# Block 0's causal taps: products summed by TensorE with the identity, halo rows dropped, orders laid out anew

## The chip, the cores and the metric

The kernel runs on one core of a Trainium2 chip, in one launch. The metric is the device time of that core in microseconds. Three runs of the kernel before gave 284.77, 285.18 and 283.43 us, the median 284.77.

The engines that matter are TensorE (PE in the profile: matmuls out of SBUF into PSUM, with PEld for its weight loads), VectorE (DVE: elementwise work), ScalarE (ACT: copies out of PSUM, activations), GpSimd (POOL) and SyncE (SP: it issues nearly all DMAs).

## What is computed

The inputs are q, k, v of 2048 rows by 640 channels, four taps per channel (`shift_k`, 640 by 4), a long filter per channel (`ssm_k`, 640 by 2048) and the weights of a gated feed-forward layer (640 by 1728). Cut to what matters here:

```python
k_shift = jnp.zeros_like(k)
for t in range(ks):                      # ks = 4, k_pad: three zero rows ahead of k
    k_shift = k_shift + k_pad[:, t:t + S, :] * shift_k[:, ks - 1 - t]
kv = k_shift * v                         # the part that the change touches
y = causal_convolution(kv, ssm_k)        # by rfft2/irfft2 in the reference
y = y + kv * ssm_D
h = q + layernorm(q) * y
out = h + (silu(n @ w_gate) * (n @ w_up)) @ w_down      # n = layernorm(h)
```

Row s of `k_shift` is the sum over jj = 0..3 of row s - jj of k times tap jj; rows before the first are zero.

## The kernel before

The 2048 rows are cut into four blocks (j = 0..3) of 512 and the 640 channels into two halves (c = 0, 1) of `CW` = 320. In a block, partition p holds rows 4p to 4p + 3, as four slots b of 320 columns.

For each (j, c), `kv_block` makes the tap sum times v. The k tile of 7 slots holds three halo slots ahead of the four (the last three rows of partition p - 1), so that row 4p + b - jj is slot 3 + b - jj of the same partition. `mul2` forms two taps' products in one VectorE instruction of 2560 columns (`kvn`), `mul1` one of 1280 (`kvs`), `add2` adds 1280 columns (`kva`), and a last multiply by v writes over the v tile (`kvv`). For block 0 the halo comes in two extra transfers per half (`kin0ch`), and GpSimd zeroes the three slots of partition 0 (`kz`).

Block 0 is then convolved by dense matrices: `ktr` turns the filter over on TensorE and `kte` copies it out, `dadd` adds D; `dfK` and `dfX` are eight 320-column matmuls each, for four h per half (the forward transform of the filter and of kv), evacuated by `deK`/`deX` on ScalarE; `m1`, `m2`, `cr`, `ci` are the products on VectorE; `di` (eight matmuls per h) sums the inverse in four PSUM banks; `w` (ScalarE) and `h` (VectorE) form the residual, `bn`, `ag`, `va` and GpSimd's `nr` the second layer norm. Only then come `hn` (the normalised rows), their transposes `tr0` and copies `te0`, and the first feed-forward matmuls `gu0`. Later blocks are convolved in two stages (`s1`, `s2`, `i2`, `i1`), and their first stages are filled in between block 0's work.

The taps: a transfer brings 2560 values into one partition of zeroed rows (`WP`), a matmul with ones spreads them over the partitions (`tapm`, four pairs of 320 columns), and four copies write them to `TAPS` (`tap`). Matmuls on ones (`warm`) and on the identity (`fill`), 512 columns wide, compute nothing; `WARM` and `FILL` say how many.

The program's order is not found at run time: `_PLAN` is a table that gives each operation its engine, its place in that engine's queue and its buffer slots, and for some transfers another one whose landing must be awaited before they are issued. Each engine works strictly through its own queue. PSUM has eight banks; a pair of banks takes one `dfK` or `dfX`, four banks one half's `di`.

## Time and profile before

| | us |
|---|---|
| median of three runs | 284.77 (283.43 to 285.18) |
| the profiled execution's own time | 285.63 |
| its span, first to last instruction | 282.8 |
| TensorE busy in the span | 268.2 (95%) |
| VectorE busy | 232.1 (82%) |
| ScalarE busy | 198.1 (70%) |
| GpSimd busy | 16.0 (6%) |

So 2.8 us of the profiled time lie around the span, and it is 0.86 us above the median. Times below are counted from the span's start. A row of the timeline gives start, length, engine, line, operation and how many instructions are merged, and in brackets the idle time ahead of it and what ended it. A row of a group gives the count, the busy time, the mean duration in ns and the idle time before. Nearly every matmul is issued at line 514, and nearly every VectorE product or sum at line 736, since helpers record them; they are told apart by their tile's shape and their place in the order. A matmul's duration there is its latency: in a row of them the next starts long before the last has ended.

### The profile page before, as it was taken

Reading aid. Unit: us, or ns where it says so; the run is one execution under the profiler, and the core shown is the slowest. Engines: PE = TensorE matmul, PEld = TensorE weight load, DVE = VectorE, ACT = ScalarE, POOL = GpSimd, SP = SyncE. Lnnn points to the kernel's source line nnn. Section 1 sums busy time; section 2 is a strip of 40 time slices with the busy share of each in tenths; the row PEclk is TensorE's granted clock in tenths of the full one; section 3 lists DMA queues with packets and bytes.
Section 4 is the critical chain, followed back from the end, with each engine's and each line's share of the span. In section 5 each row is a group of like instructions: output and inputs, shape, how many; then the busy total and the mean of one; then the engine's idle time right before and its main releaser. Section 6 shows DMA issues by size and latency. Waiting matters only on the chain.

```text
span 282.8 us, 4764 instructions
## 1 busy us (share of the span) xinstructions
PE 268.2 (95%) x1694; PEld 146.5 (52%) x1710; DVE 232.1 (82%) x428; ACT 198.1 (70%) x322; POOL 16.0 (6%) x22
## 2 busy tenths in 40 slices
PE   8989988898999998999999999999999998999996
PEld 2557554355444476644444566544444774444574
DVE  4899999999999998999999999999996843043414
ACT  4458987979989987977999789688998821430100
POOL 3000010200000021100000202000001020000000
PEclk9999999799999999999999999999999999999999
DMA  6896896899966966568432355542012061000013
GB/s 181 252 318 164 250 282 211 259 264 257 275 185 190 314 162 195 119 192 226 141 116 93 109 153 139 163 139 95 0 68 94 27 66 52 0 0 2 0 37 126
DMA packets 55282, 41.84 MB, mean 148 GB/s; under 512 B 20256, under 2 KB 52571, under 8 KB 55260
## 3 DMA queue, kind: packets, MB, share of 16 engines
q1 hardware_dynamic: 55114, 41.51, 50.5%
q8 instruction: 13, 0.21, 0.3%
q14 instruction: 9, 0.07, 0.1%
q10 hardware_dynamic: 146, 0.04, 0.1%
HBM read 19.91 MB, written 2.62 MB: 80 GB/s over the span
## 4 chain that ended last, share of the span: by engine, by line
PE 54%; DVE 26%; DMA 8%; ACT 4%; issue 3%; SPq 2%; POOL 1%; DVEq 0%
PE ps L514 53%; DVE sb L736 21%; DMA sb<-in_A_k_dram 3%; SPq L502 2%; ACT sb L494 2%; DMA sb<-sb 2%; DMA sb<-in_B_w_down_dram 2%; DMA sb<-in_A_ssm_k_dram 1%; POOL stt L863 1%; DVE sb L1066 1%; DVE sb L1228 1%; DVE stt L846 1%; ACT sb L897 1%; ACT L1161 0%; DVE sb L877 0%
## 5 line engine op out<-in xcount | busy, mean ns | idle before, releaser
L514 PE MATMUL ps<-sb 128*128 128x320 bf16 (+2 forms) x1218 | 223.0, 336 | 7.9 <-DVE sb L736 1.5
L736 DVE TENSOR_TENSOR sb<-sb 128x1280 bf16<-128x1280 bf16 (+5 forms) x273 | 180.1, 722 | 4.5 <-ACT sb L494 2.9
L514 PEld LDWEIGHTS ps<-sb 128*128 128x128 bf16 (+1 forms) x1234 | 117.4, 98 | 100.4 <-issue 8.9
L494 ACT ACTIVATE sb<-ps 128x640 bf16<-128x640 f32 (+2 forms) x160 | 112.1, 753 | 23.8 <-PE ps L514 18.8
L514 PE MATMUL ps<-sb,tab 128*128 128x320 bf16 (+2 forms) x432 | 55.2, 307 | 3.4 <-ACT sb L1161 1.0
L1161 ACT ACTIVATE sb<-ps 128x1024 bf16<-128x1024 f32 (+2 forms) x32 | 29.1, 917 | 33.3 <-PE ps L514 33.1
L514 PEld LDWEIGHTS ps<-sb,tab 128*128 128x128 f16 (+2 forms) x432 | 25.8, 102 | 30.3 <-issue 13.6
L736 DVE TENSOR_TENSOR sb<-ps,sb 128x1024 bf16<-128x1024 f32 (+2 forms) x14 | 12.6, 913 | 21.2 <-ACT sb L1161 12.1
L863 POOL TENSOR_TENSOR stt<-stt 128x2 f32<-128x2 f32 (+1 forms) x12 | 13.4, 1117 | 212.7 <-DVE stt L862 203.6
L1062 ACT ACTIVATE sb<-ps,stt 128x320 f32<-128x320 f32 x32 | 17.9, 624 | 3.3 <-PE ps L514 1.8
L1066 DVE SCALAR_TENSOR_TENSOR sb<-sb,stt 128x320 bf16<-128x320 bf16 x32 | 16.5, 543 | 0.4 <-ACT sb L1062 0.4
L1228 DVE SCALAR_TENSOR_TENSOR sb<-ps,stt,sb 128x640 bf16<-128x640 f32 x12 | 10.4, 880 | 5.4 <-PE ps L514 5.2
L897 ACT ACTIVATE sb<-sb,stt 128x640 uint8<-128x640 bf16 x16 | 13.4, 835 | 1.1 <-DVE stt L893 1.1
L890 ACT ACTIVATE sb<-sb 128x640 uint8<-128x640 bf16 x16 | 11.8, 740 | 0.4 <-DMA sb<-in_A_q_dram 0.3
L1203 DVE SCALAR_TENSOR_TENSOR sb<-ps,stt,sb 128x320 bf16<-128x320 f32 x8 | 4.1, 547 | 9.5 <-PE ps L514 9.5
L915 ACT ACTIVATE sb<-sb,stt 128x640 uint8<-128x640 bf16 x12 | 9.9, 827 | 1.2 <-DVE stt L910 0.9
L878 ACT ACTIVATE sb<-sb,stt 128x640 bf16<-128x640 bf16 x8 | 7.2, 916 | 0.3 <-DVE stt L870 0.2
L846 DVE BATCH_NORM_STATS2 stt<-sb 128x6 f32<-128x320 bf16 x8 | 3.7, 477 | 0.0
L877 DVE TENSOR_SCALAR sb<-sb,stt 128x640 bf16<-128x640 bf16 x8 | 3.5, 442 | 0.2 <-DMA sb<-sb 0.2
L495 DVE CAST sb<-ps 128x640 bf16<-128x640 f32 x1 | 0.8, 825 | 3.0 <-PE ps L514 3.0
L897 ACT ACTIVATION_READ_ACCUMULATOR sb<-sb,stt 128x1 f32 x16 | 3.3, 206 | 0.0
L890 ACT ACTIVATION_READ_ACCUMULATOR sb<-sb 128x1 f32 x16 | 3.2, 203 | 0.0
(27 smaller groups left out, 26.2 us busy)
## 6 DMA issues: line engine op xcount, KB each, us to landing
sb<-sb SPq DMA_DIRECT2D x72, 160.0 KB, 2.7
sb<-in_A_k_dram SPq DMA_DIRECT2D x6, 560.0 KB, 4.3
sb<-in_A_v_dram SPq DMA_DIRECT2D x8, 320.0 KB, 4.5
sb<-in_A_q_dram SPq DMA_DIRECT2D x8, 320.0 KB, 3.5
sb<-cst_den SPq DMA_DIRECT2D x8, 256.0 KB, 4.5
sb<-sb SPq DMA_DIRECT2D x24, 80.0 KB, 2.6
out_dram<-sb SPq DMA_DIRECT2D x12, 160.0 KB, 1.9
sb<-in_B_w_down_dram SPq DMA_DIRECT2D x3, 480.0 KB, 5.0
```

What stands on the lines that cost most here:

```text
L494: fns = {"act": lambda a: a.activation(out=dst(), in_=src(), func=ACTF.Copy), "dve": lambda v: v.tensor_copy(out=dst(), in_=src())}
L514: return lambda t: t.matmul(o(), l(), r(), start=st, stop=sp)
L736: return lambda v: v.tensor_tensor(out=o(), in0=a(), in1=b_(), op=op)
L863: P.op({"pool": 1.05}, lambda g: g.tensor_tensor(out=y, in0=va, in1=stt[:, oCO + 4:oCO + 4 + hi - lo], op=ALU.pow), c1 + [(ST, "half")], c ...
L878: "act": lambda a: a.activation(out=dst(), in_=src(), func=ACTF.Identity, scale=rs(l, j, b), bias=tmv(l, j, 3)[:, b:b + 1])},
L890: P.op({"act": act_c(D) + 0.22}, lambda a, b=b, jt=jt: a.activation(out=JU(jt), in_=V(xt, b * D, D), func=ACTF.Copy, accum_out=tmv(l, j, 4 ...
L897: P.op({"act": act_c(D) + 0.3}, lambda a, b=b, jt=jt: a.activation(out=JU(jt), in_=V(xt, b * D, D), func=ACTF.Square, bias=tmv(l, j, 5)[:, ...
L915: P.op({"act": act_c(D) + 0.3}, lambda a, b=b, jt=jt: a.activation(out=JU(jt), in_=V(xt, b * D, D), func=ACTF.Square, bias=tmv(l, j, 5)[:, ...
L1062: P.op({"act": act_c(CW, True)}, lambda a, k=k, b=b, wt=wt: a.activation(out=VF(wt, CW), in_=B32(pt, k, CW), func=ACTF.Identity, scale=tmv ...
L1066: vec(dve1(CW), lambda v, b=b, wt=wt, xv=xv: v.scalar_tensor_tensor(out=xv(), in0=xv(), scalar=tmv(0, j, 5)[:, b:b + 1], in1=VF(wt, CW), o ...
L1161: P.op({"act": act_c(n)}, lambda a: a.activation(out=dst(), in_=src(), func=ACTF.Silu), rd, wr, -1000, name=f"si{j}{i}")
L1228: vec(dve1(640), lambda v: v.scalar_tensor_tensor(out=hv(), in0=B32x2(pt, CW), scalar=tmv(0, j, 5)[:, b:b + 1], in1=hv(), op0=ALU.subtract ...
```

## The change

The shifted sum of block 0 is taken over by TensorE. Two `kvn` per half form all four taps' products from the four slots, with no shift. Then 16 matmuls per half add them up in four PSUM banks, in two groups `kvp` of eight 320-column matmuls (taps 0 and 1, then taps 2 and 3). The stationary operand is the identity where the row wanted lies in the same partition, and the identity moved by one column where it lies in the partition before (6 of 16 matmuls); the moved one starts one column ahead of the identity, in 16 columns that GpSimd zeroes (`iz`), and so gives partition 0 a zero. Two `kvv` per half multiply 640 columns from PSUM with v.

```diff
-            tm = [P.tile(f"t{j}{c}{i}", "PP") for i in range(3)]
+            tm = [P.tile(f"t{j}{c}{i}", "PP") for i in range(3 if j else 4)]
...
+                k0, st = ((3 - jj) * CW, -CW) if j else (3 * CW, 0)
...
-            if (j, c) == (0, 0):
-                mul1(0, tm[0])
-                mul1(1, tm[1])
-            else:
+            if j == 0:
                 mul2(0, tm[0], tm[1])
+                mul2(2, tm[2], tm[3])
+                pts = [Pair(f"pkv{i}") for i in range(2)]
+                for half in range(2):
+                    ms = [(b, jj) for jj in (2 * half, 2 * half + 1) for b in range(4)]
+                    ms.sort(key=lambda x: x[0] < x[1])
+                    fns = []
+                    for b, jj in ms:
+                        wrap = 1 if b < jj else 0
+                        fns.append(mm(lambda b=b: B32(pts[b // 2], b % 2, CW), lambda wrap=wrap: sb[:, IDN.base - wrap:IDN.base - wrap + 128],
+                                      lambda b=b, jj=jj, wrap=wrap: V(tm[jj], (b - jj + 4 * wrap) * CW, CW), jj == 0, jj == 3))
+                    pe(fns, CW, 8, [(tm[2 * half], 0), (tm[2 * half + 1], 0), (IDN, 0), (IDN, "z")], [(pt, "*") for pt in pts], prio, name=f"kvp{j}{c}")
+                for i in range(2):
+                    x = lambda i=i: V2(vt, 2 * i * CW, CW, 2, CW)
+                    kv_last[j, c] = vec(dve1(2 * CW), tt(x, lambda i=i: B32x2(pts[i], CW), x, ALU.mult), [(pts[i], "*"), (vt, i)],
+                        [(vt, i)], prio, name=f"kvv{j}{c}")
+                return
+            mul2(0, tm[0], tm[1])
```

With it go, for block 0, the two halo transfers of each half and GpSimd's `kz`:

```diff
-                P.op({"pool": 0.9}, lambda g: g.memset(V(kt, 0, 3 * CW, 0, 1), 0.0), [], [(kt, "z")], prio, name="kz")
...
-                dma([halo(16, 128), halo(1, 16)], 246, [], [(kt, "h")], prio, name=f"kin{j}{c}h", eng=LE)
```

The taps come in two transfers of 1280 values, one for each half of the channels, and each half's spreading matmuls wait for its own transfer (`tapck`: half c, k = 0 for taps 0 and 1, k = 1 for taps 2 and 3). The idle matmuls go from 6 + 8 + 6 times 2 to 5 + 4 + 5 times 2, and `ktr` no longer waits for the second `warm`:

```diff
-    WARM = [6, 8]
-    FILL = 6
+    WARM = [5, 4]
+    FILL = [2, 2, 2, 2, 2]
...
-        dma([(lambda: V(WP[0], 0, 8 * CW, 0, 1), lambda: dram(A_shift_k, 0, [[8 * CW, 1], [1, 8 * CW]]))], 5, [], [(w, 0) for w in WP], -3010, name="taps", eng=TAPQ)
+        for c in range(2):
+            dma([(lambda c=c: V(WP[2 * c], 0, 4 * CW, 0, 1), lambda c=c: dram(A_shift_k, c * 4 * CW, [[4 * CW, 1], [1, 4 * CW]]))], 3, [],
+                [(WP[2 * c], 0), (WP[2 * c + 1], 0)], -3010 + c, name="taps", eng=TAPQ)
...
+        P.op({"pool": 0.2}, lambda g: g.memset(sb[:, IDZ:IDZ + 16], 0.0), [], [(IDN, "z")], -3020, name="iz")
...
-            pe(fns, 128, 19, [(kr, 0), (IDN, 0)], [(pt, "*")], prio, reserve=[(kt, 0)], name=f"ktr{j}{c}", mode=3, after=held)
+            pe(fns, 128, 19, [(kr, 0), (IDN, 0)], [(pt, "*")], prio, reserve=[(kt, 0)], name=f"ktr{j}{c}", mode=3)
```

Last, `_PLAN` is a new table, and every queue has a new order, in all four blocks. Read out, the queues begin so (K0h0 stands for dfK0h0, and so on; the digit after K, X, i is the half):

```
TensorE before: warm6 tapm tapm tapm tapm warm8 ktr00 ktr01 K0h0 K0h3 X0h0 K1h0 X0h2 K0h2 K1h2 X0h1 K0h1 K1h1 X0h3 di0h0 X1h2 X1h1 K1h3 X1h0 di0h1 ...
TensorE after:  warm5 tapm11 tapm01 tapm10 tapm00 ktr00 warm4 kvp00 ktr01 kvp00 K0h0 kvp01 kvp01 X0h0 X0h1 K0h1 K0h3 X0h3 X0h2 K0h2 X1h1 di0h0 X1h0 K1h1 K1h0 di0h1 ...
VectorE before: tap0 kvs00 kvs00 kva00 kvn00 kva00 dadd kvn01 kva00 dadd kvv00 kva01 kvn01 kvn10 m1000 kva10 cr000 kvn10 kva01 m2000 kva10 kva01 ci000 m1002 kvv01 ...
VectorE after:  tap01 tap10 kvn00 kvn00 kvn01 dadd kvn01 dadd kvv00 kvv00 gz kvn10 kva10 kvv01 kvn10 m1000 m1001 kvv01 cr000 m2001 kva10 m2000 cr001 ci000 l0m0 ...
ScalarE before: ident taps | tap1 tap3 tap2 kte00 kte01 deK0h0 deX0h0 deK1h0 deK0h3 l0s02 deX0h2 ...
ScalarE after:  ident taps1 taps0 | tap00 tap11 kte00 kte01 l0s00 l0s01 deK0h0 deX0h0 deX0h1 deK0h1 l0s02 ...
SyncE before:   kin00h kin00o kraw00 kraw01 drow den-f0 kin01h kin01o den-f3 vin00 den-f2 kin10 ...
SyncE after:    kraw00 kin00o kin01o drow kraw01 vin00 den-f0 x00 den-f1 kin10 vin01 den-i1 den-f3 ...
```

In the new table `kraw01` is issued when `kraw00` has landed and `den-f0` (the first quarter of the dense matrices) when `kin01o` has. PSUM banks: `kvp00` takes 0, 1, 4, 5; `kvp01` takes 2 and 3 (after `kte01`) and 4 and 5 (after the first `kvv00`). Up to the second layer norm's last `va` VectorE has the same operations in both tables, but for the tap products and sums, one more tap copy, the memset `gz`, and one more of the small `l1m0`. Up to the first `gu0` TensorE has the same, but for `kvp`, one `fill`, and four stage-two groups of block 1 (`s2X10h1`, `s2X11h0`, `s2X11h1`, `s2X11h2`) that stood ahead of it before and stand behind it now. The first feed-forward matmuls follow `tr00`, `tr01` and one `s1` group; `te00` is copied by ScalarE and no longer by VectorE.

More of the change, by code (lines that the diff above doesn't have):

```diff
@@ L547, in bass_sequential_preLN__ssm_conv_h3__swiglu_ffn__prompt_kernel, with tap, rhs @@
         tapms = []
-        for k in range(4):
-            def tap(k):
-                pt = Pair("ptap")
-                def rhs(i):
-                    x = sb[:, WP[2 * i].base + k:WP[2 * i].base + k + 1]
-                    return bass.AP(x.tensor, x.offset, [list(x.ap[0]), [4, CW]])
-                fns = [mm(lambda i=i: B32(pt, i, CW), lambda: V(ONE, 0, 128), lambda i=i: rhs(i), True, True) for i in range(2)]
-                tapms.append(pe(fns, CW, 2, [(w, 0) for w in WP] + [(ONE, 0)], [(pt, "*")], -2800 + k, name="tapm", after=first))
-                evac(lambda: V2(TAPS, k * D, CW, 2, CW), lambda: B32x2(pt, CW), D, [(pt, "*")], [(TAPS, k)], -2800 + k, name="tap%d" % k)
-            tap(k)
-        held = [warm(WARM[1], -2790, tapms)] if WARM[1] else []
-        for _ in range(FILL):
-            warm(2, -2700, [], IDN, "fill")
+        for c in range(2):
+            for k in range(2):
+                def tap(c, k):
+                    pt = Pair("ptap")
+                    def rhs(i):
+                        x = sb[:, WP[2 * c].base + 2 * k + i:WP[2 * c].base + 2 * k + i + 1]
+                        return bass.AP(x.tensor, x.offset, [list(x.ap[0]), [4, CW]])
+                    fns = [mm(lambda i=i: B32(pt, i, CW), lambda: V(ONE, 0, 128), lambda i=i: rhs(i), True, True) for i in range(2)]
+                    tapms.append(pe(fns, CW, 2, [(WP[2 * c], 0), (WP[2 * c + 1], 0), (ONE, 0)], [(pt, "*")], -2800 + 2 * c + k, name="tapm", after=first))
+                    evac(lambda: V2(TAPS, 2 * k * D + c * CW, D, 2, CW), lambda: B32x2(pt, CW), D, [(pt, "*")], [(TAPS, (c, k))], -2800 + 2 * c + k, name=f"tap{c}{k}")
+                tap(c, k)
+        if WARM[1]:
+            warm(WARM[1], -2790, tapms[:2])
+        for n in FILL:
+            warm(n, -2700, [], IDN, "fill")
         kins, vins, kraws, xts, kts = {}, {}, {}, {}, {}
```

134 lines of the change are left out of this document (65 added, 69 removed).

## The prediction, made blind

> **What bounds the kernel now.** I read the page's busy sums, then busy time by stages, cut at four marks of block 0: its first forward matmuls of kv (15.48 us), the end of its last inverse group (47.11), the window in which the granted clock was low, and the first feed-forward matmuls (58.93).
>
> ```profile
> PE 268.2 (95%) x1694; PEld 146.5 (52%) x1710; DVE 232.1 (82%) x428; ACT 198.1 (70%) x322; POOL 16.0 (6%) x22
> ...
> core 0: us, PE busy (x) PEld busy (x) DVE busy (x) ACT busy (x) POOL busy (x), PEclk, DMA share, GB/s
> 0.00:15.48 15.48, 12.65 (x62) 5.95 (x63) 10.13 (x16) 6.46 (x7) 2.59 (x10) 1.00 0.78 229
> 15.48:47.11 31.63, 30.10 (x210) 19.60 (x212) 31.56 (x60) 25.55 (x47) 1.18 (x1) 1.00 0.86 250
> 47.11:51.02 3.91, 2.45 (x25) 0.98 (x24) 3.91 (x8) 3.87 (x8) 0.00 (x0) 1.00 0.47 134
> 51.02:54.43 3.41, 3.28 (x17) 1.17 (x16) 2.99 (x15) 3.02 (x6) 1.59 (x2) 0.50 1.07 342
> 54.43:58.93 4.50, 3.42 (x38) 1.78 (x35) 4.40 (x9) 4.20 (x7) 0.36 (x1) 1.00 0.85 223
> 58.93:282.80 223.87, 216.30 (x1352) 117.01 (x1366) 179.13 (x325) 154.99 (x250) 10.24 (x9) 1.00 0.43 124
> ```
>
> The reader is to see two full engines. From 15.48 to 47.11 VectorE has 31.56 of 31.63 us and TensorE 30.10. After 58.93 TensorE has 216.30 of 223.87 us, so what is left there is TensorE's own work. The change gives TensorE work and takes VectorE's, in the one stretch where both are full. The chain of waits shows how the stretch begins: two k transfers, then VectorE without a break.
>
> ```profile
> 1.75 3.91 DMA sb<-in_A_k_dram
> ...
> 7.06 5.15 DMA sb<-in_A_k_dram
> ...
> 12.24 1.54 DVE sb L736 x2
> ```
>
> **VectorE's account.**
>
> ```profile
> 5.88 4.87 DVE L736 TENSOR_TENSOR sb<-sb 128x1280 bf16<-128x1280 bf16 x5
> ...
> 12.24 14.01 DVE L736 TENSOR_TENSOR sb<-sb 128x2560 bf16<-128x2560 bf16 x19 [0.89 <-DMA sb<-in_A_k_dram]
> ...
> L736 DVE TENSOR_TENSOR sb<-sb 128x1280 bf16<-128x1280 bf16 x150 | 116.7, 815 | 0.2
> L736 DVE TENSOR_TENSOR sb<-sb 128x640 bf16<-128x640 bf16 x72 | 33.1, 482 | 0.3 <-ACT sb L494 0.3
> L736 DVE TENSOR_TENSOR sb<-sb 128x2560 bf16<-128x2560 bf16 x15 | 22.2, 1483 | 1.0 <-DMA sb<-in_A_k_dram 0.9
> ...
> L736 DVE TENSOR_TENSOR sb<-ps,sb 128x512 bf16<-128x512 f32 x4 | 2.7, 686 | 0.9 <-PE ps L514 0.9
> ...
> L495 DVE CAST sb<-ps 128x640 bf16<-128x640 f32 x1 | 0.8, 825 | 3.0 <-PE ps L514 3.0
> ...
> L1138 DVE MEMSET sb<- 64x256 uint32 x1 | 0.3, 272 | 0.1
> ```
>
> Removed: in half 0 two single products, three adds and a multiply of 1280 columns (6 x 0.815) and a double product (1.483), 6.37 us; in half 1 two double products and 4 x 0.815, 6.23 us; together 12.6. Added: four double products, 5.93 us, and four multiplies of 640 columns from PSUM. No row has that shape; 512 columns from PSUM take 0.686, a 640-column cast from PSUM 0.825, so 0.69 and 0.90 are the bounds and I take the nearer row, 0.82: 3.3 us. That saves 3.4 us. One more tap copy (0.83) and the memset moved ahead (0.27) give 1.1 back. In a row of instructions the next begins about 0.07 before the last ends (4 + 8 + 4 + 3 instructions of the 19 at 12.24 sum to 15.3 us in the groups and took 14.01), so I use steps of 1.41, 0.74 and 0.41 us.
>
> **TensorE's account.**
>
> ```profile
> 1.05 7.19 PE L514 MATMUL ps<-sb 128*128 128x512 bf16 x22 [1.05 <-DVE sb L528]
> 8.07 3.13 PE L634 MATMUL ps<-sb 128*128 128x128 bf16 x24
> 11.40 1.26 PE L514 MATMUL ps<-sb 128*128 128x320 bf16 x8 [0.20 <-DVE sb L736]
> 12.89 1.26 PE L514 MATMUL ps<-sb 128*128 128x320 bf16 x8 [0.23 <-DMA sb<-cst_den]
> 15.48 10.77 PE L514 MATMUL ps<-sb 128*128 128x320 bf16 x78 [1.33 <-DVE sb L736]
> ...
> L514 PEld LDWEIGHTS ps<-sb 128*128 128x128 bf16 (+1 forms) x1234 | 117.4, 98 | 100.4 <-issue 8.9
> ...
> L514 PE MATMUL ps<-sb 128*128 128x320 bf16 (+1 forms) x184 | 27.6, 303 | 2.6 <-DVE sb L736 1.3 <-ACT sb L494 1.0
> ...
> 56.59 0.73 PE L514 MATMUL ps<-sb,tab 128*64 128x320 bf16 x8
> ```
>
> 78 matmuls of 320 columns in 10.77 us, the last one's latency taken off, make 0.136 each, 1.09 for a group of eight. Added: 32, 4.35 us. Removed: seven 512-column idle matmuls, 0.22 each by the same pace, the first at half of it (22 matmuls took 7.19 us): 1.7 us. So TensorE has 2.6 us more to do, and the change gains only what TensorE's waits shrink beyond that. The weight loads of the moved identity are hidden as all of them are (0.098, busy 52%); the lower bound is zero, since a load cannot give time, and uncovered the 12 moved ones would cost 1.2 us. I take zero, by that row.
>
> **The head, walked through.**
>
> ```profile
> 0.72 1.69 SPq L502 DMA_DIRECT2D sb<-in_A_k_dram  x3
> 2.46 2.36 SPq L502 DMA_DIRECT2D sb<-in_A_ssm_k_dram  x4
> ...
> 1.76 0.51 ACTq L502 DMA_DIRECT2D sb<-in_A_shift_k_dram  x1
> ...
> 4.57 0.70 ACT L494 ACTIVATE sb<-ps 128x640 bf16<-128x640 f32 x1 [0.99 <-PE ps L514]
> ...
> 9.69 1.24 ACT L494 ACTIVATE sb<-ps 128x1280 bf16<-128x1280 bf16 x1 [2.69 <-PE ps L634]
> ```
>
> Transfers. The filter's two issues go first, 0.6 each, so k's half 0 is issued at 1.95 instead of 1.75 and lands near 5.9 by its 3.91; half 1 near 7.1 instead of 12.21. The issues of four halo transfers and 0.48 MB are gone. `kraw01` is held until `kraw00` lands (about 4.4), `vin00` and `den-f0` stand behind it and come near 10 and 11.5, ahead of their use below. `kin10` waits for its buffer, 9.5, and holds `vin01` and three dense pieces; those are wanted from 18 us on. The hidden cost is zero, and a late `den-f0` would cost its delay.
>
> Taps. Two transfers, issued near 1.4 and 1.95 after two memsets each, land near 3.4 and 4.0 by the one of before (1.76 to the first tap matmul at 3.81). The order puts the second transfer's matmuls second and fourth, and ScalarE's first copy `tap00` waits for the fourth pair: four pairs at the slow pace (0.57) end at 5.9, the copy at 6.6. VectorE's two copies end before. So the first double product starts at 6.65, where VectorE began at 5.88 before: a loss of 0.77, bounded by 0.2 and 1.3 for the landing.
>
> VectorE then runs 6.65, 8.06, 9.47, `dadd`, 11.1, `dadd`, and is free at 12.8; the first multiply from PSUM follows, then the second at 13.6, done at 14.35.
>
> TensorE: `ktr00` after the taps, `warm` to 8.2, `kvp00` 9.3, `ktr01` (1.55, half of the row of 24) 10.85, `kvp00` 11.95, K0h0 13.05. `kvp01` wants PSUM banks 4 and 5, free at 13.6: a wait of 0.55, and everything is queued behind it, ScalarE's and VectorE's next operands too. It ends at 15.8, so X0h0 starts 0.3 later than before, with K0h3 (1.09) still to do.
>
> So at 19 us VectorE has done 3.9 us more than before (at 19.0 before, two adds and the multiply of half 1 were open, 2.2 us; after, one PSUM multiply, 0.8, with a `kva`, a `kvn` and the memset done in advance, 2.5), and TensorE 1.4 us less.
>
> **From there to the feed-forward.** TensorE's 13 groups run without a wait to 30.0 as far as I can follow operands and banks. Before, 31.63 us from 15.48 on less 22 groups (24.0), 12 first-stage groups of two matmuls (3.3) and four `fill` (1.7) leave 2.6 us of waits. (The row of 184 shows 2.6 too, but with the 1.33 at the mark in it, and it counts a wait from the end of a matmul's latency.) They end on VectorE and on ScalarE; with VectorE 3 us earlier I leave 0.8 of them. Remaining: 10 groups (10.9), 11 first-stage groups of two (3.0), one `fill` (0.43), 0.8: the last inverse group ends at 45.1, against 47.11, 2.0 earlier.
>
> ```profile
> 48.02 0.54 DVE L1066 SCALAR_TENSOR_TENSOR sb<-sb,stt 128x320 bf16<-128x320 bf16 x1
> ...
> 52.60 0.24 DVE L862 TENSOR_SCALAR stt<-stt 128x2 f32<-128x2 f32 x2
> ...
> 52.85 1.95 POOL stt L863 x2
> ...
> 56.85 0.95 ACT sb L878
> ...
> 57.11 0.81 DVE L495 COPY sb<-ps 128x1280 bf16<-128x1280 bf16 x1
> ...
> 58.93 1.27 PE L514 MATMUL ps<-sb 128*128 128x256 bf16 x10
> ```
>
> From that end to the first `h` of half 1 (48.02) and to `va` (52.60) the steps are the same, with one more batch statistic behind the `h`: `va` at 50.2. Then GpSimd's powers (1.95 for two), `hn`, transposes. Before, the feed-forward began 6.3 after `va`, since it stood behind the second pair of rows (0.95 on ScalarE, then `tr01`). After, ScalarE makes one `hn` and VectorE three, with longer work between; `tr01` comes 4.5 after `va`, first matmuls 5.5 after it: 55.7, 3.2 earlier.
>
> **The remainder.** Behind that mark TensorE has its 223.9 us and the four stage-two groups that stood ahead before, 0.3 each by the eight matmuls at 56.59: 1.2 us. Other new orders there I cost at zero: the work is the same, and the waits left (7.6 us of idle in the last stage) can go either way.
>
> Sum: 282.8 - 3.2 + 1.2 = 280.8 span, and 2.8 around it: 283.6 against the profiled 285.63. That execution is 0.86 above the median; against the median of 284.77 the forecast is **282.8 us**. The same by TensorE's waits: 1.0 saved up to 15.8, 1.8 to the inverse, 1.7 before the feed-forward, less 2.6 of work.
>
> **Rivals.** *The lead passes whole.* VectorE has 179 of the last 224 us and the chain of waits gives it 26% of the span. If its queue sets the pace after block 0 too, its 3.4 to 3.9 us come through, and TensorE's 1.2 find cover: 284.8 - 3.6 = 281.2, and to 279.5 if new orders also take a third of the 7.6 us. Against it: TensorE's 97% there.
>
> *The clock falls at the wrong place.* The granted clock was 0.50 from 51.02 to 54.43, after a stretch in which TensorE was busy for 2.45 of 3.91 us, while it had little to do. The new order leaves fewer groups to fill that wait. A low window of 3.4 us across the first feed-forward matmuls costs at most its half: 282.8 + 1.7 = 284.5. The Trainium skill, "TensorE: Matmul & The Clock Gate", Part 1, says that an idle window of about 3.4 us halves the clock and that the windows run freely; the width agrees with 51.02 to 54.43, but TensorE was not idle in the 3.9 us before.
>
> *TensorE pays in full.* This one ends slower: if waits after 15.8 do not shrink, because TensorE and not VectorE was the real bound there, the 2.6 us of added work and the 0.55 wait at `kvp01` stand bare: 284.8 + 3.15 = 287.9. For it: 30.10 of 31.63. Against: VectorE's 31.56 of the same. It decides where those waits shrink by less than 0.3 us.
>
> **How the numbers follow.** Forecast 0.38 (282 to 284), clock 0.14, whole lead 0.36, full payment 0.12. About 1% is what a measurement here can tell from no change: 281.9 to 287.6. Faster is the whole lead, 0.36; slower the full payment, 0.12; within, 0.52. The range, 279.8 to 286.8, reaches into the first and short of the last; the likeliest one's own is 282 to 284.
>
> **What would show it.** First double product on VectorE near 6.65; X0h0 near 15.8 behind a wait for VectorE at `kvp01`; last inverse group near 45.1; first feed-forward matmul near 55.7; TensorE's busy time up by 2 to 3 us. Wrong would be a feed-forward start near 58, a tap copy later than 7, or new waits of some us behind the feed-forward's weights.

## The result, and the profile after

The changed kernel took 282.81 us in the median of 22 runs (280.83 to 285.93), the kernel before 284.25 us in 22 runs on the same chip (282.62 to 285.65). The ratio is 0.9945, with a 95% interval of 0.9923 to 0.9967: 0.5% faster, and within the 1% that the prediction called no change. Ratios here and below leave out single runs more than 1.5% above the fastest of their kernel. The forecast was 282.8. That the median meets it to a hundredth is luck: the forecast stood on the 284.77 of three runs, and its lead of 2.0 us came out at 1.4 here (1.6 by the ratio), and at 0.6 (1.2) when the same kernel ran again on another chip. The profiled execution took 284.94 us around a span of 283.1, 2.1 us above its median.

The page of the changed kernel, its busy sums and the group of the second-stage matmuls (helpers have moved by a line, so matmuls now stand at line 515 and VectorE's products at 737):

```profile
PE 272.1 (96%) x1735; PEld 149.4 (53%) x1735; DVE 229.8 (81%) x424; ACT 197.1 (70%) x321; POOL 13.9 (5%) x21
...
L515 PE MATMUL ps<-sb,tab 128*64 128x320 bf16 (+2 forms) x432 | 51.9, 302 | 3.6 <-DMA sb<-sb 2.6
```

and the same group before:

```profile
L514 PE MATMUL ps<-sb,tab 128*128 128x320 bf16 (+2 forms) x432 | 55.2, 307 | 3.4 <-ACT sb L1161 1.0
```

VectorE has 2.3 us less than before. TensorE's sums can't be subtracted: the page of before has 1694 matmuls to 1710 weight loads, so 16 records are missing there, and this one has 1735 of each. The second row says something new: the second-stage matmuls, which read what a shuffle DMA brings (sb to sb), wait 2.6 us for such transfers, where before ScalarE ended most of their waiting.

The same execution by stages, cut at the same marks as before: block 0's first forward matmuls of kv, the end of its last inverse group, the first feed-forward matmuls. The columns are those of the prediction's first table.

```profile
0.00:18.79 18.79, 16.82 (x82) 8.27 (x83) 11.77 (x16) 7.19 (x10) 0.98 (x9) 1.00 0.82 243
18.79:48.58 29.79, 29.17 (x212) 19.89 (x209) 28.41 (x57) 23.14 (x42) 1.18 (x1) 1.00 0.75 201
48.58:59.66 11.08, 7.43 (x65) 3.27 (x63) 10.26 (x31) 10.35 (x18) 1.37 (x2) 1.00 0.91 262
59.66:283.10 223.44, 218.66 (x1383) 118.02 (x1382) 179.37 (x323) 156.42 (x253) 10.39 (x9) 1.00 0.42 125
```

All marks are late: 18.79 for a forecast of 15.8, 48.58 for 45.1, 59.66 for 55.7. The last is beyond the "near 58" that the prediction named as a sign of being wrong. Yet a run described below, `pe180`, is the same program up to 181 us, and its profile has the first two on the forecast:

```profile
0.00:15.62 15.62, 14.12 (x81) 7.65 (x82) 10.96 (x16) 7.31 (x10) 0.98 (x9) 1.00 0.79 235
15.62:44.87 29.25, 28.91 (x212) 20.15 (x209) 29.00 (x57) 23.34 (x42) 1.18 (x1) 1.00 0.84 232
44.87:57.69 12.82, 8.64 (x65) 3.91 (x63) 10.29 (x31) 10.66 (x18) 1.37 (x2) 0.87 0.85 238
57.69:284.40 226.71, 220.08 (x1381) 119.68 (x1398) 179.62 (x323) 156.31 (x253) 10.38 (x9) 1.00 0.41 123
```

| | forecast | profile after | `pe180` |
|---|---|---|---|
| first forward matmuls of kv | 15.8 | 18.79 | 15.62 |
| from there to the end of the last inverse group | 29.3 | 29.79 | 29.25 |
| from there to the first feed-forward matmul | 10.6 | 11.08 | 12.82 |
| the rest | 225.1 | 223.44 | 223.2 (226.71 less 3.5 put in) |

So the sum came out right, 280.8 against 280.9 in the last column, though its last two terms did not: one is 2.2 us too short, the other 1.9 too long, and that they cancel is luck. The two columns differ in another way: the third row of `pe180` has a granted clock of 0.87, because the clock stood at 0.50 from 50.4 to 53.8 us, and that of the first profile has 1.00. And the first term varies by 3.2 us between executions of one program. The experiments take these one by one.

Where the head's 3.2 us come from stands in TensorE's timeline of the two executions, first the changed kernel:

```profile
4.87 1.86 PE L515 MATMUL ps<-sb 128*128 128x320 bf16 x6 [0.62 <-DMA sb<-in_A_shift_k_dram]
6.61 2.06 PE L635 MATMUL ps<-sb 128*128 128x128 bf16 x12
8.61 4.02 PE L515 MATMUL ps<-sb 128*128 128x512 bf16 x12
12.42 1.77 PE L635 MATMUL ps<-sb 128*128 128x128 bf16 x12
```

and `pe180`:

```profile
5.52 1.71 PE L635 MATMUL ps<-sb 128*128 128x128 bf16 x12
7.15 2.15 PE L515 MATMUL ps<-sb 128*128 128x512 bf16 x12
9.14 1.58 PE L635 MATMUL ps<-sb 128*128 128x128 bf16 x12
10.65 2.35 PE L515 MATMUL ps<-sb 128*128 128x320 bf16 x16
```

The reader is to compare equal rows. The same twelve matmuls (four `warm` and eight `kvp00`) take 4.02 us in one and 2.15 in the other: half the clock. The column of granted clock doesn't show it (1.00 in both heads), as a clock that has not yet risen for the first time leaves no record (the first record of this execution starts at 13.06 us); the lengths of the rows do. In the first head the taps' second transfer came late, TensorE stood 0.62 us for it, and the clock rose only at 13.06; whether the one caused the other is not shown. The late rise delays the second `ktr` (12.42 for 9.14), its copy and `dadd`, and on VectorE, whose queue is strict, the first `kvv` stands behind `dadd`, 1.99 us idle:

```profile
15.50 0.31 DVE L737 TENSOR_TENSOR sb<-sb 1x320 bf16<-1x320 bf16 x1 [1.99 <-ACT sb L495]
15.74 1.54 DVE L737 TENSOR_TENSOR sb<-ps,sb 128x640 bf16<-128x640 f32 x2
```

### The profile page after: what moved, and what is told of

Read it like the earlier page. It is cut to its first block, busy times and chain, and to the rows that moved or that the text cites. A ratio compares the mean times of both kernels' runs of the same rounds, so it can differ in the third digit from the quotient of the medians.

```text
span 283.1 us, 4820 instructions
## 1 busy us (share of the span) xinstructions
PE 272.1 (96%) x1735; PEld 149.4 (53%) x1735; DVE 229.8 (81%) x424; ACT 197.1 (70%) x321; POOL 13.9 (5%) x21
## 4 chain that ended last, share of the span: by engine, by line
PE 68%; DVE 16%; ACT 7%; DMA 4%; issue 2%; SPq 2%; POOL 1%; ACTq 0%; DVEq 0%; POOLq 0%
PE ps L515 66%; DVE sb L737 16%; ACT sb L495 4%; DMA sb<-sb 3%; SPq L503 2%; PE ps L635 1%; DMA sb<-in_A_shift_k_dram 1%; ACT sb L1074 1%; ACT sb L1173 1%; ACT L1173 0%; POOL stt L864 0%; DVE sb L1240 0%; ACT sb L879 0%; ACT sb L891 0%; DVE sb L1215 0%
## 5 line engine op out<-in xcount | busy, mean ns | idle before, releaser
L515 PE MATMUL ps<-sb 128*128 128x320 bf16 (+2 forms) x1259 | 228.9, 337 | 3.6 <-DVE sb L529 1.1
L737 DVE TENSOR_TENSOR sb<-sb 128x1280 bf16<-128x1280 bf16 (+5 forms) x264 | 174.3, 723 | 6.1 <-ACT sb L495 4.8
L515 PEld LDWEIGHTS ps<-sb 128*128 128x128 bf16 (+1 forms) x1259 | 120.4, 98 | 98.2 <-issue 8.7
L515 PE MATMUL ps<-sb,tab 128*64 128x320 bf16 (+2 forms) x432 | 51.9, 302 | 3.6 <-DMA sb<-sb 2.6
L515 PEld LDWEIGHTS ps<-sb,tab 128*64 128x64 f16 (+2 forms) x432 | 25.8, 102 | 28.5 <-issue 9.6
L737 DVE TENSOR_TENSOR sb<-ps,sb 128x1024 bf16<-128x1024 f32 (+3 forms) x18 | 15.9, 891 | 26.2 <-PE ps L515 19.6
L1240 DVE SCALAR_TENSOR_TENSOR sb<-ps,stt,sb 128x640 bf16<-128x640 f32 x12 | 10.6, 880 | 3.3 <-PE ps L515 3.2
L879 ACT ACTIVATE sb<-sb,stt 128x640 bf16<-128x640 bf16 x7 | 6.4, 915 | 0.4 <-DVE stt L871 0.2
L496 DVE CAST sb<-ps 128x640 bf16<-128x640 f32 x2 | 1.6, 819 | 3.5 <-PE ps L515 3.5
L635 PE MATMUL ps<-sb 128*128 128x128 bf16 (+1 forms) x24 | 3.8, 263 | 0.0
L635 PEld LDWEIGHTS ps<-sb 128*128 128x128 bf16 (+1 forms) x24 | 2.2, 120 | 2.3 <-issue 1.4
```

What stands on the lines that cost most here:

```text
L515: return lambda t: t.matmul(o(), l(), r(), start=st, stop=sp)
L635: return t.transpose(B16(pt, b // 2, (b % 2) * CW + d * 128, pr), src, V(IDN, 0, pr, 0, pr))
L737: return lambda v: v.tensor_tensor(out=o(), in0=a(), in1=b_(), op=op)
L1240: vec(dve1(640), lambda v: v.scalar_tensor_tensor(out=hv(), in0=B32x2(pt, CW), scalar=tmv(0, j, 5)[:, b:b + 1], in1=hv(), op0=ALU.subtract ...
```

## The experiments

Twelve kernels were run beside the kernel before, four or fewer on one chip at a time. The unaltered changed kernel stands at a ratio of 0.9945 and, in the first series here, 0.9959.

### First series: which engine sets the pace of block 0

`again` is the changed kernel unaltered.

> The changed kernel once more, unaltered. In its first profile the granted clock rose only at 13.06 us (before the change: 6.65), and block 0's first forward group of kv began at 18.79 instead of the 15.8 that was forecast. If the rise comes at a different moment in each execution (theory 'clock'), this profile can show another one, and the time goes with it: a rise at or before 9.7 us puts that group at 16 to 17 us and the time near 281; a rise near 13 puts it near 18.8 and the time near 284. If the rise does not matter (rival), the group starts near 18.8 again and the time is 282.8 give or take 0.5 whatever the clock.

It took 284.19 us (282.12 to 286.7; before 284.77 on that chip), ratio 0.9959 (0.9926 to 0.9992). Its profile, like the first, has a late clock in the head (first forward matmuls at 17.52) and the feed-forward at 59.53. The head is 1.3 us shorter than in the first profile and the span is not (283.5 for 283.1): the clock stood at 0.50 from 51.5 to 54.9 us.

`warm9` lengthens the idle matmuls ahead of the taps:

```diff
-    WARM = [5, 4]
+    WARM = [9, 4]
```

> Nine idle matmuls instead of five ahead of the tap matmuls, so that they fill the wait for the two tap transfers (3.37 to 4.87 us in the first profile). Theory 'clock': TensorE is then busy without a break from 1.05 us, the clock rises at the next boundary, by 8.3 us at the latest, the first forward group of kv starts at 16 to 16.5 us, and the time falls by 1 to 2 us against the unaltered one, to about 281.3, with fewer executions above 283. Rival 'taps': the head waits for the tap copies and VectorE whatever the clock; the first double product stays near 7.5 and the time is the same within 0.5 us. Second rival: the four added matmuls push the taps back, and it gets slower by up to 0.5 us.

283.83 us, ratio 0.9965 (0.994 to 0.999): the same as `again`. The clock was up by 6.7 us, but the tap matmuls, queued behind the idle ones, began at 4.87 instead of 3.35, and the first forward matmuls came at 17.30 against 17.52. What the clock gave, the queue took.

`dve16` cuts block 1's four double products, which lie between 16 and 40 us, into 16 pieces each, so that VectorE has 4.15 us more to do:

```diff
+                if j == 1:
+                    def piece(i, b, q):
...
+                    vec(dve2(2 * W4), [piece(i, b, q) for i in range(2) for b in range(4) for q in (0, 160)],
+                        [(kt, 0), (TAPS, (c, jj // 2))], [(a_, 0), (b_, 0)], prio, name=f"kvn{j}{c}")
+                    return
```

> VectorE's load in block 0 raised alone: the four double products of block 1 (between 17 and 32 us, wanted by TensorE only from 33 us on) are cut into 16 instructions of 160 columns each with the same result. That adds some 1.1 us to each, 4 to 5 us in all, and nothing to TensorE. If VectorE sets the pace of block 0 (the rival 'the lead passes whole'), the time rises by the whole 4 to 5 us. If TensorE sets it since the change (forecast), VectorE's lead of 3 to 4 us takes most of it and the time rises by 0 to 1.5 us.

288.09 us, ratio 1.0075 (1.0041 to 1.011): 3.9 us above `again` (3.3 by the ratios). Part of this price is the clock's. In its profile TensorE stands 2.38 us for VectorE, and a window at half the clock follows:

```profile
36.47 0.72 PE L515 MATMUL ps<-sb,tab 128*128 128x320 bf16 x4 [2.38 <-DVE sb L737]
...
37.50:40.92 3.42, 3.42 (x15) 1.95 (x14) 2.86 (x7) 2.86 (x6) 1.18 (x1) 0.50 0.63 177
```

By their mean granted clock 11 of its 12 runs have such a window and four of them two; of `again`'s 12 runs seven have one, one of them two.

`pe33` puts 16 more idle matmuls, 3.5 us, on TensorE at 33 us:

```diff
-    FILL = [2, 2, 2, 2, 2]
+    FILL = [2, 2, 2, 2, 18]
```

> TensorE's load in block 0 raised alone: the idle group at 33 us gets 18 matmuls of 512 columns instead of 2, 16 x 0.22 = 3.5 us. If TensorE sets the pace of block 0 since the change (forecast, and the rival 'TensorE pays in full'), 2.5 to 3.5 us of it come through. If VectorE still sets it, TensorE's waits up to the layer norm take most of it and the time rises by 0 to 1.5 us.

287.09 us, ratio 1.0049 (1.0017 to 1.0081): 2.9 us above `again` (2.6 by the ratios). So most of the work added to either engine between 16 and 45 us is paid for, VectorE's partly by way of TensorE's clock. The second stage's rows above fit: in `pe180` TensorE is busy 28.91 and VectorE 29.00 of 29.25 us.

### Second series: the wait before the feed-forward, the taps, the rest of the program

TensorE between the last inverse group and the feed-forward in the changed kernel's profile:

```profile
51.01 0.46 PE L515 MATMUL ps<-sb,tab 128*64 128x320 bf16 x4 [1.62 <-DMA sb<-sb]
...
53.16 1.98 PE L515 MATMUL ps<-sb,tab 128*64 128x320 bf16 x16 [0.76 <-DMA sb<-sb]
...
59.66 2.61 PE L515 MATMUL ps<-sb 128*128 128x256 bf16 x21
```

It waits twice for shuffles. SyncE's queue shows where they stand (start, time on the queue, line, operation):

```profile
43.96 1.43 SPq L597 DMA_TRANSPOSE sb<-in_A_ssm_k_dram  x1
45.44 0.58 SPq L503 DMA_DIRECT2D sb<-in_B_w_up_dram  x1
46.06 0.46 SPq L503 DMA_DIRECT2D sb<-in_B_w_gate_dram  x1
46.56 5.12 SPq L503 DMA_DIRECT2D sb<-sb  x8
```

The view of transfers gives the median time from issue to landing for those issued from 44 to 51 us. In the changed kernel:

```profile
sb<-sb SPq DMA_DIRECT2D x4, 160.0 KB, 4.6
sb<-in_B_w_up_dram SPq DMA_DIRECT2D x1, 256.0 KB, 4.3
sb<-in_B_w_gate_dram SPq DMA_DIRECT2D x1, 256.0 KB, 4.4
```

and in the kernel before, where no weights were issued right ahead of them:

```profile
sb<-sb SPq DMA_DIRECT2D x6, 160.0 KB, 2.2
```

Two things hang on the shuffles besides TensorE: VectorE's first filter product of block 1 (`kf102`) stands in its queue ahead of the normalised rows `hn`, and ScalarE's copies of the second stage (`e2K`) ahead of `hn00`. So `shfirst` issues the four shuffles ahead of both weight loads; one load follows right behind them, the other after the next eight transfers:

```diff
         P.plan(_PLAN)
+        q = P.order["sp"]
+        a, b = q[35], q[36]          # wu03, wg13; q[37:41] are shK10, q[41:45] shk11
+        q[35:50] = q[37:41] + [a] + q[41:49] + [b] + q[49:50]
```

> The changed kernel with one thing moved on SyncE's queue: the four shuffle transfers of block 1's first filter group (shK10) and the four behind them are issued ahead of two weight loads (wu03, wg13) that stood in front of them. Theory A (the feed-forward waits for these shuffles, and they are slow because the new order puts weight loads of 384 and 256 KB right ahead of them): in the changed kernel they were issued at 46.6 to 48.4 and landed after 4.4 to 4.7 us, at 51.0 to 53.1, where the shuffles issued at 41.4 to 43.3 took 2.3 to 2.7. Here they land after some 3 us, TensorE's s2K10h1 starts at about 49.3 instead of 51.0, kf102 about 1.5 us earlier, the feed-forward's first product at 58 to 58.6 instead of 59.7 (a profile whose marks before 45 us match), and the time is 1 to 1.5 us below the changed kernel's 284.2 of the first series. Rival B (the transposing load issued at 44.0, which stays in front, is what slows them): they still take over 4 us, the marks and the time stay within 0.4 us. Rival C (the shuffles land earlier, but the weights of the feed-forward's first product, wg00, landed at 58.1 and now land later, and take over the wait): s2K10h1 early, first product not, time unchanged or up to 0.5 us worse.

282.77 us (before 284.80 in this series), ratio 0.9934 (0.9905 to 0.9964), 1.4 us under `again`. The same row in its view of transfers:

```profile
sb<-sb SPq DMA_DIRECT2D x3, 160.0 KB, 2.2
```

The four that were moved, issued from 42.5 to 44.9 us, took 2.2 too. The shuffles land twice as fast, with the transposing load still in front, so B falls and A's mechanism holds. (Both weight loads are of 256 KB by these rows; the expectation has 384 for one.) A's time is not shown: against the changed kernel's own 0.9945 and 0.9959 the gain is 0.3 to 0.7 us by the ratios, within the intervals.

The feed-forward began 10.5 us after the last inverse group's end (55.24 after 44.77), where `pe180`, with the same head and the old order, needed 12.82. Most of these 2.3 us is not the landing but the clock, since `pe180` had its low window there. `onetap`, described next, has the old order and no low window in its profile; first its row of this stage, then that of `shfirst`:

```profile
45.23:56.08 10.85, 7.33 (x64) 3.29 (x62) 10.26 (x31) 10.35 (x18) 1.57 (x2) 1.00 0.89 264
44.77:55.24 10.47, 7.36 (x65) 3.36 (x63) 10.26 (x31) 10.29 (x18) 1.68 (x2) 1.00 0.86 256
```

So the earlier landing by itself is worth 0.4 us here, and 0.6 against the first profile's 11.08. What else the moved shuffles did is in the granted clock of the runs: a mean under 0.996, that is a low window of some 3.4 us, have 17 of the changed kernel's 34 runs, 7 of the 12 of `onetap` and 8 of the 12 of `pe180`, the last two on the same chip as `shfirst`, and none of the 12 of `shfirst`. Then TensorE waited again, from 57 to 74 us:

```profile
PE ps L515 <- DMA sb<-sb: 1.7, 1, 1.7
PE ps L515 <- ACT sb L1173: 0.8, 1, 0.8
```

A wait of 1.7 us, for the next filter group's shuffles (shK11), which neither `pe180` nor the first profile has in these microseconds, took more than the landing had brought.

`onetap` brings the taps in one transfer again:

```diff
-        for c in range(2):
-            dma([(lambda c=c: V(WP[2 * c], 0, 4 * CW, 0, 1), ...
+        dma([(lambda: V(WP[0], 0, 8 * CW, 0, 1), lambda: dram(A_shift_k, 0, [[8 * CW, 1], [1, 8 * CW]]))], ...
```

> The changed kernel with the taps in one transfer again, as before the change; all else as changed. Theory A (the second transfer's late landing holds TensorE and VectorE at the head, and the gaps keep the granted clock low): all four tap products start between 3.4 and 5.3 without a wait, the first double product at about 6.4 instead of 7.3 to 7.6, the clock rises at about 6.7 instead of 10.5 or 13.1, block 0's first transform of the values (dfX0h0) starts at about 16 instead of 17.5 to 18.8, and, as both engines set the pace of block 0, the time falls by 0.8 to 1.6 us against the changed kernel. Rival B (the first product waits for k, which lands at 5.8 to 6.2, and for VectorE's two tap copies anyway): first product within 0.4 us of 7.3, time within 0.4 us. Rival C (the lead is there at 16 us but is lost before 45 us in waits for tables and values): dfX0h0 early, the last inverse product (di1h3) still at 45.3 or later, time within 0.4 us.

283.77 us, ratio 0.9972 (0.9936 to 1.0008): within 0.4 us of `again`. In its profile the one transfer brought the first tap matmul at 3.88, behind a wait of 0.51 us, and none waited after it; of two, the first gave 3.21 to 3.41 where the clock was early, and the second was mostly there in time. First double product at 7.16, first forward matmuls at 16.29. Theory A's mark for the first forward matmuls came, its time did not; rival B had the size right. A gain or loss by the split is not shown.

`pe180` puts the 16 idle matmuls at 181 us:

```diff
-    FILL = [2, 2, 2, 2, 2]
+    FILL = [2, 2, 18, 2, 2]
```

> The changed kernel with 16 more idle matmuls of 512 columns on TensorE at about 181 us (3.5 us at the full clock), in the middle of a later block's feed-forward, where nothing else is changed. Theory A (after block 0 TensorE alone sets the end, so whatever starts the feed-forward earlier passes through to the end): time 3.0 to 3.6 us above the changed kernel. Rival B (later waits, for transfers or VectorE, would absorb part of a lead too): at most 2.5 us above. With the same load at 33 us the time rose by 2.9.

285.96 us, ratio 1.0057 (1.0027 to 1.0087). Against the unaltered kernel's 0.9945 to 0.9959 that is 2.8 to 3.2 us: four fifths or more pass through, nearer to A, though the intervals (up to 0.9 us to either side of each) do not exclude B's 2.5. TensorE sets the pace there for the most part.

`warm54` is the kernel of before with the changed kernel's idle matmuls in the head:

```diff
-    WARM = [6, 8]
+    WARM = [5, 4]
```

> The kernel of before with the head's idle matmuls cut to the changed kernel's numbers (5 and 4 in place of 6 and 8), nothing else. The prediction counted this cut as 1.1 us less TensorE work at the head. Theory A (VectorE's chain sets the head of the old kernel, so the cut is worth nothing there): time within 0.5 us of before, dfX0h0 at 15.5. Rival B (the cut by itself brings the gain): 0.8 to 1.2 us below before. Rival C (fewer idle matmuls keep the granted clock low for longer): the clock rises at 10 us or later in place of 6.7 and the time is 0.5 to 2 us above.

286.72 us, ratio 1.0059 (1.0027 to 1.0092): 1.7 to 1.9 us slower, which none of the theories had with its reason. The clock rose in good time, the first forward matmuls came earlier than before (14.76 against 15.48), and so did everything up to 99 us (a row of matmuls at 99.3 against 100.2). The lead was lost, and more, at 117 us. ScalarE in that profile:

```profile
119.21 0.92 ACT L878 ACTIVATE sb<-sb,stt 128x640 bf16<-128x640 bf16 x1 [2.02 <-DMA sb<-sb]
```

and TensorE, which stands for ScalarE's copies:

```profile
120.86 2.22 PE L514 MATMUL ps<-sb,tab 128*64 128x320 bf16 x16 [1.62 <-ACT sb L494]
```

An earlier TensorE met a transfer within SBUF that was not there yet, and ScalarE, strict in its order, passed the wait on; a low clock window from 122.3 to 125.7 us followed. That is the reading of one profile, and was not tried apart.

### Third series and the last run: the next shuffles, and block 0's two loads

`sh2` moves, besides, two of the next shuffles ahead of a weight load:

```diff
+        q[56:60] = q[58:60] + q[56:58]     # shK11G3, shK11G2 ahead of wg10, shk20
```

> The changed kernel with both sets of shuffles moved ahead on SyncE's queue: those of the run before this one (block 1's first filter group ahead of wu03 and wg13), and two of the second filter group (shK11G3, shK11G2) ahead of wg10 and one shk20, behind which they were issued at 62.7 and 63.9 in that run and landed after 4.4 and 3.8 us; TensorE stood still for 1.7 us from 66.0 for the last of them, which took back most of the 2 us by which the feed-forward began earlier. Theory A (each gain is given back at the next transfer that stands behind weight loads, and goes away with it): the wait of 1.7 us falls below 0.5, gu020 starts about 1.3 us nearer to gu000, and the time is 1 to 1.7 us under that run's 282.8. Rival B (wg10, now issued 1.3 us later, becomes the next wait): the wait moves to the products of the second pair, and the time stays within 0.4 us of 282.8. Rival C (the rest of the program waits for something that stands at its own time, and the gain is lost after 75 us): the wait at 66 us is gone and the time within 0.4 us all the same.

282.23 us (281.23 to 283.23; before 284.40 in this series), ratio 0.9918 (0.9886 to 0.9949). TensorE's waits from 57 to 74 us:

```profile
PE ps L515 <- ACT sb L1173: 0.8, 1, 0.8
PE ps L515 <- ACT sb L495: 0.8, 1, 0.8
```

No shuffle is waited for any more, and the feed-forward group `gu020` came 12.3 us after the first feed-forward matmul instead of about 14. Again no run has a low window (none of 6, against 8 of 11 of `kvp5` and 11 of 12 of `dveless`, below, on the same chip). The time fell less than expected, by 0.5 us or, as a ratio, 0.2%. The chain of waits of this execution names what came next, a load of q that stood behind them all on SyncE's queue:

```profile
66.99 0.59 SPq L503
67.62 3.44 DMA sb<-in_A_q_dram
71.09 0.05 ACT sb L891
...
71.92 2.70 ACT sb L495 x4
```

So rival B's kind of answer, with another transfer than it named; by its size rival C is met as well. `sh2` has the lowest ratio of the versions that leave nothing out, and is clearly quicker than the kernel before; over the changed kernel (0.9945 and 0.9959) its lead is within the intervals.

`kvp5` leaves out 11 of the 16 product matmuls per half, `dveless` most of VectorE's second double products:

```diff
-                    ms = [(b, jj) for jj in (2 * half, 2 * half + 1) for b in range(4)]
+                    ms = [(b, 2 * half) for b in (range(3, 4) if half else range(4))]
```

```diff
-                mul2(2, tm[2], tm[3])
+                vec(dve2(16), tt(lambda: V(tm[2], 0, 16), lambda: V(kt, 3 * CW, 16), lambda: V(TAPS, 2 * D + c * CW, 16), ALU.mult),
+                    [(kt, 0), (TAPS, (c, 1))], [(tm[2], 0), (tm[3], 0)], prio, name=f"kvn{j}{c}")
```

> The changed kernel with 5 of the 16 product matmuls of each channel half of block 0: tap 0 for all four row groups and tap 2 for one. It leaves out 22 matmuls of 0.136 us, 3.0 us of TensorE; VectorE's work is as it was. Adding 3.5 us to TensorE at 33 us raised the time by 2.9, adding 4.2 us to VectorE by 3.9. Theory A (in block 0 the two engines are even, each just in the other's shadow: work added to either is paid, work taken from one alone is not): time within 1.0 us of the changed kernel's 284.2. Theory B (TensorE's sum is on the path, as the rival that lets TensorE pay in full has it): 2.3 to 3.0 us below. Theory C (TensorE and VectorE stand in one chain, one after the other): 1.2 to 2.3 us below.

> The changed kernel with VectorE's second double product of each channel half of block 0 cut to 16 columns (about 0.16 us in place of 1.49), so taps 2 and 3 are summed from the products of taps 0 and 1; TensorE's matmuls are as they were. VectorE loses 2.7 us of work before 14 us. Theory A (the engines are even, TensorE in the shadow of VectorE no more than 1 us away): time within 1.0 us of the changed kernel's 284.2, with TensorE's waits in block 0 gone. Theory B (VectorE alone sets block 0's end): 2.0 to 2.7 us below. Theory C (one chain through both): 1.2 to 2.0 us below.

`kvp5` took 281.98 us, ratio 0.9921 (0.9892 to 0.9951), 0.7 to 1.1 us under the changed kernel for 3.0 us of TensorE. `dveless` took 282.70, ratio 0.9941 (0.9909 to 0.9973), at most 0.5 us under it for 2.7 us of VectorE. TensorE's head in `kvp5`:

```profile
11.49 1.26 PE L515 MATMUL ps<-sb 128*128 128x320 bf16 x8 [0.65 <-DVE sb L737]
13.86 4.17 PE L515 MATMUL ps<-sb 128*128 128x320 bf16 x29 [1.11 <-DVE sb L737]
```

and in `dveless`:

```profile
9.39 1.58 PE L635 MATMUL ps<-sb 128*128 128x128 bf16 x12
10.90 7.27 PE L515 MATMUL ps<-sb 128*128 128x320 bf16 x50
```

Lighter by 3 us, TensorE stands 1.76 us for VectorE, and its first forward matmuls come at 14.59, one microsecond earlier than `pe180`'s 15.62. With VectorE lighter TensorE runs without a gap, and they come at 15.56, no earlier. So neither engine gains much alone in the head either. Both gains in time lie within the intervals of the unaltered kernel, and the low windows of both kernels may hide part of them.

`both` takes both loads off `sh2`:

> The changed kernel with the shuffles of the run before last moved ahead (both sets), and with both of block 0's loads taken off at once: 5 of 16 product matmuls (3.0 us of TensorE left out) and VectorE's second double products cut to 16 columns (2.7 us of VectorE left out; the output lacks most of the tap sums of block 0). Alone, without the moved shuffles, the first brought 1.1 us and the second 0.3 or nothing, and the shuffles moved alone stood at 282.2. Theory A (TensorE and VectorE are even in block 0, so that only taking work from both shortens it, and the shuffles then no longer swallow it): dfX0h0 at 13 to 14, di1h3 at 41.5 or earlier instead of 43.5 to 44.4, time 2 to 3 us under 282.2. Theory B (something else holds block 0 once either is lighter: the tables' transfers, ScalarE's evacuations, bank releases): di1h3 at 42.5 or later, time less than 1.4 us under 282.2.

281.40 us (279.47 to 282.93; before 284.20), ratio 0.9892 (0.9858 to 0.9926): 0.7 to 0.8 us under `sh2`, within the intervals of six runs each, so theory A's 2 to 3 us did not come, and B has the size. Its profile can't tell why, since its clock came late (TensorE stood 0.48 us for the taps, and the twelve transposes took 2.06 us): the first forward matmuls came at 16.29. From there to the last inverse group's end it has about the same stage as the others (28.9 to 30.0 us), which the cuts hardly touch:

```profile
16.29:46.12 29.83, 29.52 (x211) 19.77 (x210) 29.61 (x58) 23.45 (x43) 1.19 (x1) 1.00 0.82 224
```

What would hold the head with both loads gone and an early clock stays open.

## Why the prediction came out, step by step

- *VectorE's account* was right: 2.3 us less busy time, as 3.4 less 1.1. The multiply from PSUM, the one shape without a row, is in the groups by shape:

```profile
L737 DVE TENSOR_TENSOR sb<-ps,sb 128x640 bf16<-128x640 f32 x4 | 3.2, 811 | 0.0
```

- *TensorE's account* is confirmed in its price and not in its sum. Sixteen matmuls, the second `kvp00` and the first group behind it, take 2.35 us at 10.65 in `pe180`: 0.137 each with the last one's latency taken off, the 0.136 of the forecast, so the moved identity's loads cost nothing. The sums of the pages (268.2 before, 272.1 with a late clock, 269.9 in `sh2`) don't show the 2.6 us. `sh2` with all 1735 records is 2.6 us busier than `shfirst` with 1717, so the 16 that are missing before are worth some 2.3 us, an estimate; and before has a low window in which its rows are longer.
- *The head* was right where the clock rose in time: 15.62 in `pe180`, 15.76 in `shfirst` and 15.64 in `sh2` for 15.8, with a wait for VectorE at `kvp01` of 0.43 to 0.44 for 0.55 and the first double product at 6.49 in `pe180` for 6.65. The prediction had no term for a late rise, which put 17.52 and 18.79 in its place; in the first profile the double product began at 7.58, behind ScalarE's tap copy, which is later than the 7 that the prediction named as a sign of being wrong.
- *From there to the inverse* was right: 29.25 for 29.3, and 28.9 to 30.0 in the other profiles with unchanged work there. TensorE's waits there shrank to 0.34 us (29.25 less 28.91) from 1.53 in the same columns before, so the rival in which TensorE pays in full falls: it lived on these waits staying.
- *"First matmuls 5.5 after it"* (after `va`) is right at full clock and fails with a low window. Where this stage has none, the step measured 5.98 in the profile after, 5.7 in `onetap` and 5.3 in `pe33`, and 5.4 in `shfirst`, `sh2` and `both`; with one it measured 7.7 in `pe180`, 7.9 in `again` and 6.6 to 7.7 in three others. The prediction walked from `h` to `va`, `hn` and the transposes, and left out what stands ahead of them in each engine's queue: second-stage groups whose shuffles the new SyncE order had put behind weight loads. Waiting for them costs up to 0.6 us by itself (5.98 against 5.4); what it costs beyond that comes with the clock.
- *The clock at the wrong place* is that rival, half come true. Its chance of 0.14 was low: half of the changed kernel's runs (17 of 34) have a low window after the first rise. It is not new, since 36 of 103 runs of before have one too. Its place was wrong: in `again`'s trace it lay at 51.5 to 54.9 us, where it had been before, ahead of the first feed-forward matmuls and not across them. Its price of at most 1.7 us fits the step (1.7 us more in `pe180` than in the profile after), but of that only 0.9 us is left in the span (medians of 281.5 and 280.6 with and without one, over the runs that the ratios use). The order of the shuffles largely decides whether it comes: of the 24 runs of `shfirst`, `sh2` and `both`, which move them, one had it. The traces show TensorE busy for 1.0 to 1.95 of the 3.4 us ahead of a fall in seven kernels, and for 2.2 to 2.6 of such stretches between 44.8 and 50.4 us in `shfirst`; but the first profile, with 1.6 to 1.8 in such stretches, had no fall, so this is no rule yet.
- *The remainder*, 225.1, was the other miss, with the opposite sign: 223.4, and 223.2 in `pe180`. It began from a misreading. The 7.6 us of idle in the last stage of before hold the 16 missing records, all of which lie there; with some 2.3 us for them the idle time was about 5.3, and after it is 4.8 (223.44 less 218.66). So the waits hardly changed, TensorE was nearer to 98% than to 97%, and what did not show up is the 1.2 us for the four groups that moved in: the stage is 0.4 us shorter than the 223.87 of before. Which of the new orders made room for them was not tried.
- *The lead passes whole* fell by its own mark, 281.2, and the loads say why: TensorE is as full as VectorE up to 45 us, and it sets most of the pace after (`pe180`).

So the forecast's cause, that the lead shrinks because TensorE is full too, is supported by the loads; its exact figure is partly luck. A late head of up to 3.2 us and the low windows, neither of which the sum has, stand against a remainder that was costed 1.7 to 1.9 us too high.

## What to carry to other kernels

Where two engines are full in a stage, adding to either costs most of its price and relief of one buys little; look at the waits of the third party, here SyncE's queue. When a change reorders a queue of transfers, read for each transfer on the critical path what is issued just ahead of it: 512 KB of weights, needed much later, doubled the landing time of the four shuffles behind them. A short wait can cost more than its length when the clock falls with it: here up to 0.6 us directly, and one to two more where a low window came. And a lead won early must be followed to the next transfer that was timed for the old pace, since that is where it is lost: in these runs that was at 51, 66, 71 and 117 us.

## What was unexpected of the hardware

The start of the clock is a lottery of some 3 us. Programs with the same first 40 us gave first forward matmuls at 15.62, 15.64, 15.76, 17.52 and 18.79 us; in the late ones rows of equal matmuls took twice as long up to 10 or 13 us. In four late heads (the first profile, `again`, `dve16`, `both`) TensorE had waited 0.48 to 0.62 us for the taps; but `onetap` waited 0.51 us too, a little earlier, and its clock was up in time, so the wait alone does not decide it. The Trainium skill, "TensorE: Matmul & The Clock Gate", Part 1, says that the window in which activity is judged runs freely, so that the same kernel warms up at varying times, and puts the cost under 1% of a typical kernel span; the traces agree on the first and come to 3.2 us of 283 between the extremes, 1.1%. Part 4 of that page says that transposes don't count as busy in the same way. The late head fits: from 4.87 us on TensorE had no wait, but twelve transposes lay from 6.61 to 8.67, and the pace stayed at half beyond them. The head of `pe33` fits as well: its clock was up from 4.10 us and fell at 7.51, though TensorE had been busy for 3.13 of the 3.41 us between, with transposes from 6.14 on:

```profile
4.10:7.51 3.41, 3.13 (x19) 1.50 (x18) 1.95 (x3) 1.21 (x2) 0.00 (x0) 1.00 0.94 281
7.51:10.92 3.41, 3.41 (x13) 1.59 (x12) 3.41 (x3) 1.33 (x2) 0.00 (x0) 0.50 0.90 278
```

No run here sets transposes against other matmuls alone, so this is not shown.

A shuffle of 160 KB took 2.2 us to land without weight loads right ahead of it and 4.6 behind two weight loads of 256 KB and a transposing load, and moving only the weight loads away was enough to get 2.2 again.
